# Sharing the early decode of eight weight tiles and the low parts of four token chunks between VectorE, ScalarE and TensorE

## The chip, the cores and the metric

One core of one Trainium2 chip runs the whole program. The metric is the device time of one execution in microseconds. TensorE multiplies matrices into PSUM, VectorE and ScalarE do element-wise work, GpSimd helps with small element-wise steps, SyncE (and ScalarE's sequencer) issue the DMAs.

## The reference

A gated linear attention over 4 batches, 8 heads, 768 steps and 48 channels per head is followed by two feed-forward layers on 3072 tokens (model width 384, hidden width 2048). Cut to what matters:

```python
f = 1.0 / (1.0 + np.exp(-f_logit))
for t in range(S):                      # attention
    state = f[:, :, t, :, None] * state + k_t (outer) v_t
    y[:, :, t] = q_t @ state
x = y.transpose(0, 2, 1, 3).reshape(3072, 384)
h = np.maximum(x @ w_in, 0.0);  x = (h * h) @ w_out        # layer 0
h = x @ w_in2;  x = np.where(h > 0, h, np.exp(np.minimum(h, 0)) - 1) @ w_out2   # layer 1
```

The weights reach the chip as 64-bit floats, two 32-bit words each, and are turned into 32-bit floats there ("decode").

## The kernel before

The 3072 tokens are 24 chunks of 128 (index g), and the feed-forward layers run on 12 blocks of 512 tokens (index i, six for each layer). A block goes through 16 hidden tiles of 128 (index f). One pair (i, f) is a unit. In block 0 unit f needs weight tile f of layer 0 for the first time, so all 16 tiles of layer 0 have to be loaded, decoded and split during block 0, beside the attention of the first chunks.

Products are made in a reduced format, fp32r, with every operand split in a high part (a rounded copy made by ScalarE) and a low part (the difference, made by VectorE). `up` (L403) makes nine matmuls: for each of three k the high and the low part of the weights against the high part of x, then the high parts of the weights against the low part of x. So its second matmul already needs the low part of the weights. `down` (L464) makes six matmuls of full fp32 for tiles 0 to 7 of block 0 (their second half is split later, in `split_rest`) and nine fp32r matmuls elsewhere.

A weight tile f goes through these steps, named by the letters of START where it is issued there:

- r: `load_raw` (L350), a DMA of 768 KB into one of only two buffers, so the load of tile f waits until tile f - 2 is decoded. Tiles 0 to 2 are issued by SyncE, the later ones of layer 0 by ScalarE's sequencer.
- w: `decode_weights` (L357), which calls `decode` (L50): one pass on ScalarE (L54) and three on VectorE (L56, L59, L60).
- W: `split_weights` (L373), which calls `split` (L368): high part on ScalarE (L370), low part on VectorE (L371). For tiles 0 to 7 it covers 384 columns, from tile 8 on 768.

A chunk of attention goes through f (load of the gates), q and v (loads), g (`a_gate`: tanh on ScalarE, then a scale by ScalarE or GpSimd), d (`a_decay`: two scans on VectorE), c (`a_scale`), s (`a_scores`) or, from chunk 4 on, `a_keys` (transposes tp on TensorE), t (`a_transposed`, kt on ScalarE), `a_near` (sk on TensorE), m (`a_mask`, VectorE), `a_states`, `a_far`, `a_out`, and last h (`a_hi`, L311, ScalarE) and l (`a_lo`, L318, VectorE), the high and low part of x.

The order on every engine's queue is the order of the program, written by hand: first the string START (L34), one token a step, with U, B and L for `up`, `between` (the activation) and `low` of units 0 and 1; then a loop over units u = 2, 3, ... (L569) which at each u issues what `plan[u]` holds, then `up(u)`, `down(u - 2)`, `between(u)`. `plan` is filled by `at(slot, ...)`: first the attention steps of all chunks, then, in a loop over f (L529),

```python
    for f in range(NF):
        at(f - 3, load_raw, 0, f)
        at(f - 2, decode_weights, 0, f)
        at(f - 1, split_weights, 0, f)
        if f < WHOLE:
            at(10 + f // 2, split_rest, f)
```

so that slot u holds, in this order, the split of tile u + 1, the decode of tile u + 2 and the load of tile u + 3. In slots 10 to 13 the `split_rest` of two of the tiles 0 to 7 come before these. The tensors ds (decays), mn (a running minimum of decays that in the end decides on a fallback) and dlast (the last decay of a chunk, copied by GpSimd) belong to `a_decay` (L152).

Of the kernel before, what the change touches and what calls it, by code (L numbers as in the profile page):

```python
# [11 lines left out]
F32 = mybir.dt.float32  # L12
F32R = mybir.dt.float32r
I32 = mybir.dt.int32
U32 = mybir.dt.uint32
I64 = mybir.dt.int64
AF = mybir.ActivationFunctionType
ALU = mybir.AluOpType
# [4 lines left out]
NG = NT // 128  # L23
# [8 lines left out]


START = """f0 q0 f1 I q1 M v0 f2 v1 f3 g0 q2 d0 q3 c0 g1 v2 d1 s0 r0 c1 r1 t0 g2 k0 m0 g3 s1 t1 y0 d2 c2 h0 v3 k1  # L34
m1 s2 d3 v4 t2 y1 c3 k2 m2 s3 h1 w0 t3 l0 y2 k3 m3 W0 r2 h2 q4 w1 y3 f4 l1
l2 h3 l3 W1 g4 r3 w2 U0 B0 L0 W2 d4 U1 B1 L1 w3 r4 T f5"""
STAGED = 27
WHOLE = 8
NEAR = dict(zip(range(B, NG), (4, 6, 9, 11, 19, 21, 23, 25, *range(28, 4 * NG - 23, 4))))
# [20 lines left out]
    V.scalar_tensor_tensor(out=out, in0=lo, scalar=29, in1=out, op0=ALU.logical_shift_right, op1=ALU.bitwise_or)  # L60


def chunked(ctx, tc, ff, qk, vk, vz, wraw, mask, ident, flag, out):


# [15 lines left out]
    ps_a = ctx.enter_context(tc.tile_pool(name="ps_a", bufs=1, space=PSUM))  # L81

    idt = one.tile([128, 128], F32, name="idt")
    msk = one.tile([128, 128], I32, name="msk")
    lim = one.tile([ROWS, 521], F32, name="lim")
    mn = one.tile([ROWS, 2 * NP], F32, name="mn")
    mrow = one.tile([ROWS, 1], F32, name="mrow")
    ds = [one.tile([ROWS, 2, 521], F32, name=f"ds{i}") for i in range(2)]
    tri = one.tile([128, 120], I32, name="tri")[:, 0:64]
    ss = [wpool.tile([128, 2, NP, 128], F32, tag="w", name=f"ss{i}") for i in range(2)]  # L90
    sd = [one.tile([128, 2, NP, 64], F32, name=f"sd{i}") for i in range(2)]
    s0 = one.tile([ROWS, NP, 48], F32, name="s0")
    s1 = one.tile([ROWS, NP, 48], F32, name="s1")
    state = [one.tile([ROWS, NP, 48], F32, name=f"state{b}") for b in range(B)]
    dlast = [one.tile([ROWS, NP], F32, name=f"dlast{b}") for b in range(B)]

    one.tile([128, 16], F32, name="shift")
    gap.tile([128, 48], F32, name="shift2")
# [53 lines left out]
    def a_decay(g):  # L152


        a, f = ds[g % 2], st[g]["ff"]
        V.memset(lim[:, ::65], 1.0)
        V.tensor_tensor_scan(out=a[:, 0, 0:520], data0=f[:, 0:520], data1=lim[:, 0:520], initial=1.0, op0=ALU.mult, op1=ALU.max)
        V.reciprocal(out=lim[:, 65::65], in_=a[:, 0, 64::65])
        V.tensor_tensor_scan(
            out=a[:, 1, ::-1], data0=f[:, ::-1], data1=lim[:, ::-1], initial=1.0, op0=ALU.mult, op1=ALU.max  # L160
        )
        V.tensor_tensor(out=mn, in0=mn, in1=a[:, 0, 64::65], op=ALU.min)
        here = a[:, 0, 64::65].rearrange("r (p h) -> r p h", h=2)
        if g >= B:

            wc = two.tile([ROWS, NP], F32, tag="wc", name=f"wc{g}")
            G.tensor_tensor(out=wc, in0=here[:, :, 0], in1=dlast[g % B], op=ALU.mult)
            st[g]["wc"] = wc
        if g < NG - B:
            G.tensor_copy(dlast[g % B], here[:, :, 1])  # L170

    def a_scale(g):

# [73 lines left out]
    def a_direct(g):  # L247
        s = st[g]
        pool, tag = ((ps_a, "a1"), (ps_y, "y2"), (ps_y, "y0"), (ps_y, "y1"))[g]
        yp = pool.tile([128, NK, 128], F32, tag=tag, name=f"yp{g}")  # L250
        for k in range(NK):
            for p, c in ((k, 0), (NK, 48)):
                for j in range(2):
                    PE.matmul(  # L254
                        yp[64 * j:64 * j + 64, k], s["vz"][:, k, j, c:c + 64], ss[g % 2][:, at_(p, j), p],
                        start=c == 0, stop=c > 0,
                    )
        s["yp"] = yp

# [58 lines left out]
    def a_lo(g):  # L318
        i, o = where[g]
        hi, lo = (x[:, :, o:o + 128] for x in xr[i])  # L320
        if g < B:
            V.tensor_tensor(out=lo, in0=st[g]["yp"], in1=hi, op=ALU.subtract)  # L322
        else:
            V.tensor_tensor(out=lo, in0=st.pop(g)["x1"], in1=hi, op=ALU.subtract)

# [8 lines left out]
        V.tensor_tensor(out=lo, in0=x, in1=hi, op=ALU.subtract)  # L334

    def least_decay():
        V.tensor_reduce(out=mrow, in_=mn, axis=mybir.AxisListType.X, op=ALU.min)

    def raise_flag():
        tp = ps_a.tile([1, ROWS], F32, tag="a2", name="mt")  # L340
# [13 lines left out]
    def whole(layer, f):  # L354
        return layer == 0 and f < WHOLE

    def decode_weights(layer, f):  # L357

        if whole(layer, f):
            if f % 2 == 0:  # L360
                st["pair"] = wpool.tile([128, 2, 2 * DM], U32, tag="w", name=f"pair{f}")
            b = st["pair"][:, f % 2]
        else:
            b = two.tile([128, 2 * DM], U32, tag="dec", name=f"dec{layer}_{f}")
        decode(nc, raws[layer, f], b)
        raws[layer, f] = b

    def split(t, b):  # L368
# [125 lines left out]
    def at(slot, f, *args, to=plan):  # L494

        if slot > 1:
            to.setdefault(slot, []).append((f, args))
# [31 lines left out]
    for f in range(NF):  # L529
        at(f - 3, load_raw, 0, f)  # L530
        at(f - 2, decode_weights, 0, f)
        at(f - 1, split_weights, 0, f)
        if f < WHOLE:
            at(10 + f // 2, split_rest, f)

        at(STAGED + 4 * f, load_raw, 1, f)
        at(STAGED + 4 * f + 2, decode_weights, 1, f)
        at(STAGED + 4 * f + 5, split_weights, 1, f)
        at(16 * (n1 - 1) + f + 3, fetch_weights, f)
# [4 lines left out]
    units = [(i, f) for i in range(len(BLOCKS)) for f in range(NF)]  # L544
    with tc.manual_schedule():
        V.memset(lim, DMIN)
        V.memset(mn, 1.0)
        V.memset(ss[0], 0.0)
        G.memset(ss[1], 0.0)
        for a in sd:  # L550
            G.memset(a, 0.0)

        warm = ps_a.tile([128, 512], F32, tag="a2", name="warm")
        for _ in range(3):
            PE.matmul(warm, ss[0][:, 0, 0], ss[0][:, 0].rearrange("r p t -> r (p t)"), start=True, stop=True)
        steps = {
            "I": lambda: nc.sync.dma_start(out=idt, in_=ident),
            "M": lambda: nc.sync.dma_start(out=msk, in_=mask),
            "T": lambda: [nc.sync.dma_start(out=tri[c:c + 64], in_=mask[c:c + 64, 64 - c:128 - c]) for c in (0, 64)],
            "f": load_f, "q": load_qk, "v": load_v, "r": lambda f: load_raw(0, f),  # L560
            "g": a_gate, "d": a_decay, "c": a_scale, "s": a_scores, "t": a_transposed, "m": a_mask, "k": a_state,
            "y": a_direct, "h": a_hi, "l": a_lo,
            "w": lambda f: decode_weights(0, f), "W": lambda f: split_weights(0, f),
            "U": lambda f: up(0, f), "B": lambda f: between(0, f),
            "L": lambda f: low(0, f),
        }
        for o in START.split():
            steps[o[0]](*(int(c) for c in o[1:]))
        for u in range(2, len(units) + 2):  # L569

            last = units[u - 2] == (n1 - 1, NF - 1)
            todo = plan.get(u, ())
            for f, args in () if last else todo:
                f(*args)
            if u < len(units):
                up(*units[u])
            down(*units[u - 2])
            for f, args in (*(todo if last else ()), *behind.get(u, ())):
                f(*args)
            if u < len(units):  # L580
                between(*units[u])
                low(*units[u])
# [162 lines left out]
```

## Time and profile before

| | us |
|---|---|
| median of 3 runs | 896.77 |
| lowest and highest of these | 896.03 and 897.23 |
| the profiled execution | 895.2 |
| its span (first to last instruction) | 893.4 |

Busy time of the engines in the profiled execution: TensorE 870.5 us (97%), VectorE 565.1 us (63%), ScalarE 442.6 us (50%), GpSimd 279.8 us (31%). The span is 1.8 us shorter than the execution's own time; times below count from the start of the span. A row gives the start, the duration, the engine (PE is TensorE, PEld its weight loads, DVE is VectorE, ACT is ScalarE, POOL is GpSimd, SPq and ACTq the sequencers that issue DMAs), the line of the kernel, the operation, what is written from what, and in brackets how long the engine was idle before it and what ended that.

### The profile page before, as it was taken

What the parts mean: (1) busy time and instruction counts of PE and PEld (TensorE: products, weight loads), DVE (VectorE), ACT (ScalarE), POOL (GpSimd) and SP (SyncE); (2) the same over time, 40 slices, a digit from 0 to 9 for tenths busy, and PEclk for the clock granted to TensorE, in tenths of its full rate; (3) what the DMA queues carried; (4) which work ended last, traced back from release to release, by engine and by line L of the source; (5) the groups of instructions that cost most, each with busy time, mean ns of one, the idle gap of its engine ahead of it and who ended that gap; (6) DMA issues with size and microseconds to landing.
All of it is one profiled execution on the core that took longest, in us unless ns stands there. A gap on an engine that the chain in (4) does not pass through costs nothing.

```text
span 893.4 us, 15977 instructions
## 1 busy us (share of the span) xinstructions
PE 870.5 (97%) x6273; PEld 706.8 (79%) x6273; DVE 565.1 (63%) x857; ACT 442.6 (50%) x795; POOL 279.8 (31%) x245
## 2 busy tenths in 40 slices
PE   7799999999999999999999999999999999999996
PEld 5565788888888888888888888888888888888885
DVE  8899987778777877844331565565555655654543
ACT  3466854445445455544554444444444544454443
POOL 2101045343333333223323223333333323232321
PEclk8999999999999999999999999999999999999998
DMA  9655342424454433523586400100100100200001
GB/s 269 192 171 185 114 119 72 120 81 151 140 157 150 155 114 116 193 75 109 208 307 230 162 12 1 60 12 1 60 13 0 60 12 1 71 1 28 9 1 39
DMA packets 33778, 88.66 MB, mean 99 GB/s; under 512 B 5504, under 2 KB 10240, under 8 KB 33696
## 3 DMA queue, kind: packets, MB, share of 16 engines
q1 hardware_dynamic: 31824, 77.35, 26.3%
q10 hardware_dynamic: 1872, 10.22, 3.3%
q8 instruction: 50, 0.82, 0.4%
q14 instruction: 32, 0.26, 0.1%
HBM read 64.55 MB, written 22.02 MB: 97 GB/s over the span
## 4 chain that ended last, share of the span: by engine, by line
PE 88%; DVE 4%; DMA 3%; ACT 2%; SPq 1%; issue 1%; ACTq 0%; DVEq 0%
PE ph L413 41%; PE y L477 41%; DMA ff<-ff 2%; PE o L285 1%; SPq L296 1%; PE o L270 1%; PE tp L186 1%; DMA raw<-wraw 1%; PE sk_a L209 1%; DVE pair L60 1%; DVE pair L59 1%; PE sk_a L218 0%; PE sc L196 0%; DMA vk<-vk 0%; PE yp L254 0%
## 5 line engine op out<-in xcount | busy, mean ns | idle before, releaser
L460 POOL TENSOR_TENSOR gl<-gg,gh 128x512 fp32r<-128x512 f32 x175 | 234.2, 1338 | 457.7 <-PE ph L413 189.4
L477 PE MATMUL y<-gh,wf 128*128 128x512 f32 (+1 forms) x582 | 177.7, 387 | 0.0
L446 DVE SCALAR_TENSOR_TENSOR t<-r,t 128x512 f32<-128x512 f32 (+1 forms) x97 | 71.3, 735 | 154.5 <-ACT r L445 154.1
L477 PE MATMUL y<-gh,w 128*128 128x512 f32 x528 | 162.5, 389 | 0.0
L413 PE MATMUL ph<-xh,w 128*128 128x512 f32 x576 | 154.8, 403 | 3.4 <-ACT w L370 2.5
L442 ACT ACTIVATE r<-ph 128x512 f32<-128x512 f32 (+1 forms) x97 | 57.6, 593 | 181.8 <-PE ph L413 176.8
L413 PE MATMUL ph<-xh,wf 128*128 128x512 f32 (+1 forms) x582 | 146.4, 387 | 0.0
L413 PEld LDWEIGHTS ph<-xh,w 128*128 128x128 f32 x576 | 105.1, 189 | 28.2 <-ACT w L370 2.9
L477 PEld LDWEIGHTS y<-gh,wf 128*128 128x128 f32 x582 | 108.8, 188 | 22.3
L413 PEld LDWEIGHTS ph<-xh,wf 128*128 128x128 f32 x582 | 108.6, 188 | 22.3
L477 PEld LDWEIGHTS y<-gh,w 128*128 128x128 f32 x528 | 99.1, 188 | 20.6
L477 PE MATMUL y<-gl,wf 128*128 128x512 f32 (+1 forms) x291 | 112.6, 387 | 0.0
L477 PE MATMUL y<-gl,w 128*128 128x512 f32 x264 | 102.7, 389 | 0.0
L434 ACT ACTIVATE r<-ph 128x512 f32<-128x512 f32 x88 | 52.1, 592 | 95.6 <-PE ph L413 88.9
L413 PE MATMUL ph<-xl,w 128*128 128x512 f32 x288 | 81.5, 392 | 0.6 <-DVE xl L322 0.6
L413 PE MATMUL ph<-xl,wf 128*128 128x512 f32 (+1 forms) x291 | 81.1, 387 | 0.0
L440 DVE TENSOR_TENSOR gh<-r 128x512 fp32r<-128x512 f32 x64 | 44.0, 688 | 55.2 <-ACT r L434 51.6
L447 DVE SCALAR_TENSOR_TENSOR gg<-ph,t 128x512 f32<-128x512 f32 (+1 forms) x97 | 66.6, 686 | 10.4 <-DVE t L446 0.5
L413 PEld LDWEIGHTS ph<-xl,w 128*128 128x128 f32 x288 | 54.4, 189 | 12.8 <-DVE xl L322 1.0
L477 PEld LDWEIGHTS y<-gl,wf 128*128 128x128 f32 x291 | 54.6, 188 | 11.1
L413 PEld LDWEIGHTS ph<-xl,wf 128*128 128x128 f32 x291 | 54.4, 188 | 11.1
L444 ACT ACTIVATE t<-r 128x512 f32<-128x512 f32 (+1 forms) x97 | 61.0, 629 | 3.1
(101 smaller groups left out, 1019.1 us busy)
## 6 DMA issues: line engine op xcount, KB each, us to landing
raw<-wraw SPq DMA_DIRECT2D x19, 768.0 KB, 5.8
wst<-w SPq DMA_DIRECT2D x16, 768.0 KB, 4.3
wf<-wst SPq DMA_DIRECT2D x16, 768.0 KB, 4.6
raw<-wraw ACTq DMA_DIRECT2D x13, 768.0 KB, 4.2
ff<-ff SPq DMA_DIRECT2D x22, 227.9 KB, 4.6
k<-qk SPq DMA_DIRECT2D x22, 224.0 KB, 4.7
q<-qk SPq DMA_DIRECT2D x22, 224.0 KB, 4.8
x2d<-yo SPq DMA_DIRECT2D x18, 256.0 KB, 2.9
```

What stands on the lines that cost most here:

```text
L59: V.scalar_tensor_tensor(out=out, in0=hi, scalar=0x80000000, in1=out, op0=ALU.bitwise_and, op1=ALU.bitwise_or)
L60: V.scalar_tensor_tensor(out=out, in0=lo, scalar=29, in1=out, op0=ALU.logical_shift_right, op1=ALU.bitwise_or)
L186: PE.transpose(tp[:, p, 0:ROWS], k[:, p], idt[:ROWS, :ROWS])
L413: PE.matmul(ph, w[:, a, 0, 128 * k:128 * k + 128], b[:, k, c], start=(m == 0), stop=(m == len(todo) - 1))
L434: A.activation(r[:, c], ph, AF.Relu)
L440: V.tensor_tensor(out=gh[:, c], in0=r[:, c], in1=r[:, c], op=ALU.mult)
L442: A.activation(r[:, c], ph, AF.Relu, scale=-1.0)
L444: A.activation(t[:, c], r[:, c], AF.Tanh, scale=-0.5)
L446: V.scalar_tensor_tensor(out=t[:, c], in0=r[:, c], scalar=1.0, in1=t[:, c], op0=ALU.add, op1=ALU.mult)
L447: V.scalar_tensor_tensor(out=gg[:, c], in0=ph, scalar=0.0, in1=t[:, c], op0=ALU.max, op1=ALU.add)
L460: G.tensor_tensor(out=gl, in0=gg, in1=gh, op=ALU.subtract)
L477: PE.matmul(yp_[i][m][:, c], w[:, 128 * m:128 * m + 128], b[:, c], start=(f == 0 and n_ == 0), stop=(f == NF - 1 and n_ == 2 and c.stop == n),
```

## The change

- `decode_shared` takes the place of `decode` for tiles 0 to 7. ScalarE makes a second pass: it reads byte 3 of each low word and writes its three top bits, as an integer, back into the low word. VectorE is left with two passes: shift the first pass left by 3 and OR in these bits, then OR in the sign. The first of VectorE's three passes (L56) is gone.
- `a_lo` for chunks 0 to 3: three matmuls of 128 columns with a negated identity matrix (nid, written once by ScalarE at step N) add minus the high part to what is still in PSUM, and ScalarE copies the result. VectorE's subtraction (L322) is gone. For this `a_direct` starts its accumulation once for a whole bank.
- In `plan` the decode and load of a slot now come before its splits: slot u holds the decode of tile u + 2, the load of tile u + 3, then `split_rest`, then the split of tile u + 1. This holds for all 16 tiles of layer 0.
- START: N is new, l0 moves behind q4, l1 before y3, w1 behind y3.
- mn and dlast become one tensor, `ends`, with a column group for each chunk: VectorE copies where it took a minimum, GpSimd's copies are gone, and the minimum is taken once at the end, over 192 columns in place of 8.

```diff
-m1 s2 d3 v4 t2 y1 c3 k2 m2 s3 h1 w0 t3 l0 y2 k3 m3 W0 r2 h2 q4 w1 y3 f4 l1
-l2 h3 l3 W1 g4 r3 w2 U0 B0 L0 W2 d4 U1 B1 L1 w3 r4 T f5"""
+m1 s2 d3 v4 t2 y1 c3 k2 m2 s3 h1 w0 t3 N y2 k3 m3 W0 r2 h2 q4 l0 l1 y3 w1 f4 l2
+h3 l3 W1 g4 r3 w2 U0 B0 L0 W2 d4 U1 B1 L1 w3 r4 T f5"""
...
+def decode_shared(nc, raw, out):
+    words = raw.bitcast(U32).rearrange("p (n two) -> p n two", two=2)
+    top = raw.bitcast(U8).rearrange("p (n b) -> p n b", b=8)[:, :, 3]
+    hi, lo = words[:, :, 1], words[:, :, 0]
+    A, V = nc.scalar, nc.vector
+    A.activation(out.bitcast(F32), hi.bitcast(F32), AF.Copy, scale=2.0**-112)
+    A.activation(lo, top, AF.Copy, scale=1 / 32, bias=-31 / 64)
+    V.scalar_tensor_tensor(out=out, in0=out, scalar=3, in1=lo, op0=ALU.logical_shift_left, op1=ALU.bitwise_or)
+    V.scalar_tensor_tensor(out=out, in0=hi, scalar=0x80000000, in1=out, op0=ALU.bitwise_and, op1=ALU.bitwise_or)
...
-        V.tensor_tensor(out=mn, in0=mn, in1=a[:, 0, 64::65], op=ALU.min)
-        here = a[:, 0, 64::65].rearrange("r (p h) -> r p h", h=2)
+        V.tensor_copy(ends[:, g], a[:, 0, 64::65])
         if g >= B:
+            here, last = (ends[:, i].rearrange("r (p h) -> r p h", h=2) for i in (g, g - B))
-            G.tensor_tensor(out=wc, in0=here[:, :, 0], in1=dlast[g % B], op=ALU.mult)
+            G.tensor_tensor(out=wc, in0=here[:, :, 0], in1=last[:, :, 1], op=ALU.mult)
-        if g < NG - B:
-            G.tensor_copy(dlast[g % B], here[:, :, 1])
...
         if g < B:
-            V.tensor_tensor(out=lo, in0=st[g]["yp"], in1=hi, op=ALU.subtract)
+            yp = st[g]["yp"]
+            for k in range(NK):
+                PE.matmul(yp[:, k], nid, hi[:, k], start=False, stop=True, skip_group_check=True)
+            A.activation(lo, yp, AF.Copy)
...
-        decode(nc, raws[layer, f], b)
+        (decode_shared if whole(layer, f) else decode)(nc, raws[layer, f], b)
...
         at(f - 2, decode_weights, 0, f)
+    for f in range(NF):
         at(f - 1, split_weights, 0, f)
...
+            "N": lambda: A.activation(nid, idt, AF.Copy, scale=-1.0),
```

## Rows read from the trace of the kernel before

**Rows 1.** Busy time by stage: PE, PEld, DVE, ACT, POOL, clock, DMA share, GB/s

```profile
46.00:75.00 29.00, 28.41 (x280) 17.81 (x279) 26.90 (x46) 16.51 (x31) 4.06 (x6) 1.00 0.57 193
75.00:107.00 32.00, 29.20 (x410) 20.98 (x410) 31.27 (x52) 25.62 (x52) 1.35 (x2) 1.00 0.44 149
170.00:250.00 80.00, 80.00 (x838) 66.20 (x837) 61.23 (x91) 40.46 (x81) 33.45 (x31) 1.00 0.45 140
```

**Rows 2.** Timeline of TensorE's weight loads, one that waits for a low part

```profile
99.94 1.00 PEld L413 LDWEIGHTS ph<-xh,w 128*128 128x128 f32 x5 [0.63 <-DVE w L371]
```

**Rows 3.** Groups by shape, VectorE, 22 to 112: busy us, mean ns, idle before

```profile
L371 DVE TENSOR_TENSOR w<-pair,w 128x384 fp32r<-128x384 f32 x16 | 8.5, 553 | 1.7 <-ACT w L370 1.7
...
L56 DVE TENSOR_SCALAR pair<-pair 128x768 uint32<-128x768 uint32 x8 | 4.5, 557 | 2.4 <-ACT pair L54 2.4
...
L322 DVE TENSOR_TENSOR xl<-yp,xh 128x384 fp32r<-128x384 f32 x4 | 2.0, 548 | 0.0
```

**Rows 4.** Groups by shape, ScalarE, 22 to 112

```profile
L54 ACT ACTIVATE pair<-raw 128x768 f32<-128x768 f32 x8 | 7.2, 897 | 0.0
...
L370 ACT ACTIVATE w<-dec 128x768 fp32r<-128x768 f32 x7 | 5.9, 840 | 2.5 <-DVE dec L60 1.3 <-DVE lim L156 1.1
...
L316 ACT ACTIVATE xh<-yp 128x384 fp32r<-128x384 f32 x3 | 1.5, 485 | 1.2 <-PE yp L254 1.2
...
L245 ACT ACTIVATE state<-kv 112x192 f32<-112x192 f32 x2 | 0.7, 331 | 4.7 <-PE kv L244 4.7
```

**Rows 5.** Chain that ended last, 20 to 46, in order of time

```profile
26.66 0.33 SPq L352
...
28.16 5.44 DMA ff<-ff
...
35.09 0.57 DVE pair L56
```

**Rows 6.** Timeline of VectorE around slot 2

```profile
38.23 0.56 DVE L371 TENSOR_TENSOR w<-pair,w 128x384 fp32r<-128x384 f32 x1 [0.59 <-ACT w L370]
...
45.61 0.55 DVE L371 TENSOR_TENSOR w<-pair,w 128x384 fp32r<-128x384 f32 x1
...
47.66 0.96 DVE L60 SCALAR_TENSOR_TENSOR pair<-raw,pair 128x768 uint32<-128x768 uint32 x1
```

**Rows 7.** Timeline of TensorE, units 2 to 5

```profile
38.25 3.09 PE L413 MATMUL ph<-xh,w 128*128 128x512 f32 x6 [2.49 <-ACT w L370]
...
46.12 1.64 PE L413 MATMUL ph<-xh,w 128*128 128x512 f32 x6
...
57.51 0.57 PE L186 MATMUL tp<-idt,k 112*128 112x112 f32 x4 [0.54 <-issue]
...
63.59 0.22 PE L209 MATMUL sk_h<-q,k 48*64 48x64 f32 x1
```

**Rows 8.** Timeline of ScalarE, slot 5

```profile
58.12 0.54 ACT L231 ACTIVATE kt<-tp 128x448 f32<-128x448 f32 x1 [1.13 <-PE tp L186]
58.56 0.63 ACT L146 ACTIVATE ff<-ff 112x521 f32<-112x521 f32 x1
```

**Rows 9.** Timeline of VectorE, slots 4 to 11

```profile
57.33 0.55 DVE L371 TENSOR_TENSOR w<-pair,w 128x384 fp32r<-128x384 f32 x1
...
64.58 0.43 DVE L236 COPY_PREDICATED sd<-tri,sk_a 128x256 f32<-128x256 int32 x1
...
73.89 0.96 DVE L371 TENSOR_TENSOR w<-dec,w 128x768 fp32r<-128x768 f32 x1 [0.45 <-ACT w L370]
...
98.93 0.95 DVE L371 TENSOR_TENSOR w<-dec,w 128x768 fp32r<-128x768 f32 x1
```

**Rows 10.** Timeline of TensorE, slot 13

```profile
105.93 0.72 PE L285 MATMUL o<-sd,vk 64*48 64x64 f32 x32 [1.24 <-ACT seen L277]
```

**Rows 11.** Busy time by microsecond around unit 2; columns as in the first group

```profile
40.00:41.00 1.00, 1.00 (x4) 0.81 (x3) 0.93 (x3) 0.68 (x2) 0.70 (x2) 0.50 0.86 295
...
42.00:43.00 1.00, 1.00 (x4) 0.60 (x3) 0.96 (x2) 0.00 (x0) 0.70 (x1) 0.97 0.38 91
```

More of the change, by code (lines that the diff above doesn't have):

```diff
@@ L15 @@
 U32 = mybir.dt.uint32
+U8 = mybir.dt.uint8
 I64 = mybir.dt.int64
@@ L83, in chunked @@
     idt = one.tile([128, 128], F32, name="idt")
+    nid = one.tile([128, 128], F32R, name="nid")
     msk = one.tile([128, 128], I32, name="msk")
     lim = one.tile([ROWS, 521], F32, name="lim")
-    mn = one.tile([ROWS, 2 * NP], F32, name="mn")
+    ends = one.tile([ROWS, NG, 2 * NP], F32, name="ends")
     mrow = one.tile([ROWS, 1], F32, name="mrow")
     ds = [one.tile([ROWS, 2, 521], F32, name=f"ds{i}") for i in range(2)]
-    tri = one.tile([128, 120], I32, name="tri")[:, 0:64]
+    tri = one.tile([128, 96], I32, name="tri")[:, 0:64]
     ss = [wpool.tile([128, 2, NP, 128], F32, tag="w", name=f"ss{i}") for i in range(2)]
@@ L94, in chunked @@
     state = [one.tile([ROWS, NP, 48], F32, name=f"state{b}") for b in range(B)]
-    dlast = [one.tile([ROWS, NP], F32, name=f"dlast{b}") for b in range(B)]
     one.tile([128, 16], F32, name="shift")
@@ L255, in a_direct @@
                         yp[64 * j:64 * j + 64, k], s["vz"][:, k, j, c:c + 64], ss[g % 2][:, at_(p, j), p],
-                        start=c == 0, stop=c > 0,
+                        start=k == 0 and c == 0, stop=c > 0, skip_group_check=True,
                     )
@@ L336, in least_decay @@
     def least_decay():
-        V.tensor_reduce(out=mrow, in_=mn, axis=mybir.AxisListType.X, op=ALU.min)
+        V.tensor_reduce(out=mrow, in_=ends.rearrange("r g n -> r (g n)"), axis=mybir.AxisListType.X, op=ALU.min)
     def raise_flag():
@@ L546, in chunked @@
         V.memset(lim, DMIN)
-        V.memset(mn, 1.0)
         V.memset(ss[0], 0.0)
```

## The prediction

> **What bounds the kernel now.** I read the busy time by stage first. From 170 us on TensorE is busy all the time (80.00 of 80.00 us in the stretch shown), so what happens there at other engines costs nothing, and the change hardly touches it. Between 46 and 107 us it is different: VectorE is busy 26.90 of 29 and 31.27 of 32 us, while TensorE loses 0.6 and 2.8 us [rows 1]. The timeline of VectorE in that stretch runs without gaps but for a few waits of half a microsecond. So block 0 goes at VectorE's pace, and a microsecond that TensorE gets earlier through block 0 is kept to the end; after 107 us it can't be won any more.
>
> The second thing to see is the point of handover. `up` of a unit needs the low part of its weight tile at its second matmul, and TensorE waits for exactly that: at 99.94 a weight load waits 0.63 us for L371 [rows 2]. There are five such waits (units 2, 7, 12, 14 and 15), and in units 3 to 5 and 8 the low part ends within 0.3 us of its use, as at 45.61 + 0.55 = 46.16 against unit 3, whose first matmul starts at 46.12 [rows 6, 7]. So VectorE hands over just in time, and the order of its steps counts as much as their sum.
>
> The third is what sets the start of unit 2. The chain of waits goes: decode 0 ends, SyncE issues the load of tile 2 at 26.66, then the gates of chunk 4 at 28.16, which land after 5.44 us; the tanh on them is ahead of decode 2 on ScalarE, so VectorE gets decode 2 only at 35.09 [rows 5].
>
> **The change, part by part.**
>
> *Removed from VectorE.* Eight passes L56 of 557 ns, with the gap of 0.03 us between instructions 0.59 us each, 4.7 us in all, and four subtractions L322 of 548 ns, 2.2 us [rows 3]. Tiles 0 to 2 and the four subtractions lie ahead of unit 2, the other five passes (2.95 us) behind it.
>
> *Added on ScalarE.* Eight passes of 768 elements. No row shows a read of single bytes or a write to every second word. The nearest are L54, which reads every second word (897 ns), and L370, which does neither (840 ns) [rows 4]. The strided read costs 0.06 us, a strided write as much again at most: 0.84 to 0.95 us; I take 0.90. Four copies like L316 (485 ns) and step N, which is smaller than L245 (331 ns), are added where ScalarE waits 4.7 us for L244 in two places [rows 4]. TensorE's twelve small matmuls each move a quarter of the columns of those at 46.12 (1.64 us for six), so they are under 0.27 us each, and TensorE waits 2.49 us ahead of unit 2 [rows 7]; they are hidden, and cost at most what is left of 3.3 us were that wait gone.
>
> *Start of unit 2.* Decode 0 has no cover: its path becomes two ScalarE passes and two VectorE passes. 0.90 replaces 0.59, and ScalarE passes overlap by 0.1, so it ends 0.2 us later. The load of tile 2 and the gates of chunk 4 are queued behind it on SyncE, so the tanh comes 0.2 later, and decode 2 repeats the loss: unit 2 starts 0.39 us later (0.3 to 0.6 by the bounds). That the four subtractions are gone gains nothing, since the gates end last: VectorE waits there in either order (2.4 us ahead of L56, most of it here [rows 3]).
>
> *Order in a slot.* This is the step that counts. In slot 2 VectorE ran the low part of tile 3 (45.61 to 46.16) and then decode 4 (to 47.66 + 0.96 = 48.62) [rows 6]. One decode behind the handover is thus 2.46 us, or 1.87 without L56. Now decode 4 comes first. Low part of tile 3: 46.16 + 0.39 - 0.59 (decode 3) + 1.87 = 47.83. The second matmul of unit 3, ready at 46.12 + 0.27 before, comes 1.46 us later. From there TensorE has no slack: units 3 and 4 follow, and tp(5), which had waited 0.54 us for k at 57.51 [rows 7], now starts at 56.97 + 1.46 = 58.43, 0.92 later. On ScalarE kt(5) and the tanh of chunk 6 (58.12 and 58.56 [rows 8]) shift with it, and both are queued ahead of decode 7. So its two passes start at 58.56 + 0.92 + 0.57 = 60.05 and end at 61.75. VectorE has finished the low part of tile 5 at 57.33 + 0.55 = 57.88 [rows 9], + 0.39 - 3 x 0.59 + 1.87 = 58.37, and stands still for 3.4 us: all that the dropped passes had saved. Decode 7 and the low part of tile 6 end at 64.15, and the mask of chunk 5 needs scores that TensorE ends at 63.59 + 0.22 + 0.92 = 64.73 [rows 7], against 64.58 before [rows 9]. So at the mask VectorE stands 0.15 us behind the old kernel.
>
> From tile 8 on nothing is removed, and only the order acts: each low part comes one old decode (2.46) later. What that earns is that VectorE no longer waits for ScalarE's high part (0.45 at 73.89 [rows 9]). The low part of tile 12, which ended at 98.93 + 0.95 = 99.88 [rows 9], ends at 99.88 + 0.15 + 2.46 - 0.45 = 102.04, and unit 12 is 2.1 us late.
>
> *What is given back.* In slot 13 TensorE waited 1.24 us for ScalarE's copy `seen` [rows 10], which stood behind splits and the activation of unit 12. With TensorE 2.1 us later ScalarE is ahead of it, and I leave 0.3 of this wait, so 0.94 come back. Slot 14 has no decode left, so no further delay is added. Sum: 2.1 - 0.94, about 1.2 us later from unit 14 to the end.
>
> *The rest.* `ends`: a copy of 8 columns for a minimum of 8 columns on VectorE, one larger reduction late, beside a busy TensorE; GpSimd loses 20 small copies, and a wait is added there: wc now follows VectorE's last scan, with the gate scale of the next chunk queued behind it, which is needed only by the next scan. I cost these at nothing; were VectorE's cover gone, they would cost under 0.5 us. SyncE's and ScalarE's loads keep their order; the load in a slot is now issued ahead of the split, which can only help.
>
> **The rivals.**
>
> *VectorE's saving goes through.* If ScalarE gets decode 7 done in time (TensorE less late at tp(5)), VectorE never stands still. Then at the low part of tile 12 it has gained 2.95 us, the 0.45 above and 1.1 of its 1.7 us of waits for high parts (0.59 of these at 38.23 are ahead of unit 2 [rows 3, 6]), and lost 0.39 and the 2.46 of the order: 1.65 us earlier, up to 2.6 with the wait for `seen`. I take 2.2: 894.6 us. For it: VectorE is the bound. Against it: the handover, which is just in time already.
>
> *The clock falls again.* This one is slower. TensorE stood still for 2.49 us ahead of unit 2, and the granted clock then read 0.50, its lower level (1.2 GHz), until about 42 [rows 7, 11]; six matmuls of unit 2 took 3.09 us against 1.64 in unit 3 [rows 7]. In the forecast TensorE stands still for about 2 us ahead of unit 3's second matmul and as long in unit 7, where low part 7 now follows decode 8. If the clock falls there, each fall costs 3.09 - 1.64 = 1.45 us at most, and the first is passed on through tp(5) in full: 1.2 + 1.45, 899.4 us; with both 900.9. It decides from the point where such a pause makes the clock fall; the row shows that 2.5 us did. The Trainium skill (TensorE: Matmul & The Clock Gate, section "What's actually happening") says that the reduced clock is the default and activity lifts it, so pauses bring it back. By that rule this rival would be likely, and the trace agrees with its 0.50 behind the pause ahead of unit 2.
>
> *The change acts only in the first eight tiles.* Were the new order harmless because TensorE has slack, only the 0.39 us would be left: 897.2 us. Rows 2 speak against it. It lies in the forecast's own spread.
>
> **How the numbers follow.** The profiled execution took 895.2 us, 1.8 more than its span; plus 1.2 that makes 896.4. The median of the runs is 896.77, 1.6 above it, so I forecast 898.0 for the median. About 0.2%, 1.8 us, is what a measurement of this kernel can tell from no change. The forecast has a chance of 0.50; with its spread of about 1 us, 0.46 of it are within 0.2% and 0.04 above. The clock rival has 0.31, all of it slower. The rival in which the saving goes through has 0.19, faster. That makes faster 0.19, same 0.46, slower 0.35. The range reaches from the fast rival to both falls of the clock: 894.4 to 900.9; the forecast alone would be 897.0 to 899.0.
>
> **What would show it.** In the profile after: VectorE's busy time lower by about 6.6 us; unit 2 starts at 38.6; TensorE waits for L371 about 1.5 us in unit 3 and 2 us in unit 7; VectorE idles about 3 us ahead of decode 7, released by ScalarE; unit 14 starts about 1.2 us later. The forecast is wrong if ScalarE's new pass is much dearer than 0.95 us, if VectorE has no idle time at decode 7, or if the granted clock reads 0.50 behind 45 us.

## The result, and the profile after

| | us |
|---|---|
| median before, beside it | 896.40 (895.92 to 897.23) |
| median after | 906.54 (905.24 to 907.83, 4 runs) |
| after to before | 1.0111, interval 1.0099 to 1.0124 |
| the profiled execution after, its span | 906.96, 905.2 |

The changed kernel is about 10 us slower. The forecast was 898.0, and the range ended at 900.9.

The page of after, its span and the busy time of each engine, gives the first reading. VectorE has 4.5 us less to do than before (565.1), ScalarE 8.5 more (442.6), and TensorE is busy 6.6 us longer (870.5) with twelve small matmuls more and otherwise the same work.

```profile
span 905.2 us, 15994 instructions
PE 877.1 (97%) x6285; PEld 713.3 (79%) x6285; DVE 560.6 (62%) x844; ACT 451.1 (50%) x808; POOL 265.5 (29%) x225
```

The stages of after, with the columns of [rows 1]: from 46 to 75 us VectorE falls from 26.90 to 22.22 us of work and TensorE from 28.41 to 25.78. Most of that work isn't gone, it comes later. The stretch behind 170 us is full, as before. The granted clock, third column from the end, reads 0.94 and 0.95 where it was 1.00, and 0.93 behind 107 us. In the kernel before TensorE was full there, at 1.00, as the line behind these shows.

```profile
46.00:75.00 29.00, 25.78 (x262) 15.88 (x261) 22.22 (x39) 17.33 (x32) 1.84 (x3) 0.94 0.47 156
75.00:107.00 32.00, 29.66 (x345) 20.32 (x345) 28.76 (x47) 22.73 (x44) 1.00 (x2) 0.95 0.48 159
107.00:130.00 23.00, 18.79 (x131) 14.72 (x132) 15.03 (x23) 15.39 (x31) 0.63 (x1) 0.93 0.34 107
170.00:250.00 80.00, 80.00 (x957) 66.23 (x956) 59.42 (x93) 39.95 (x83) 29.96 (x27) 1.00 0.41 129
```

```profile
107.00:130.00 23.00, 22.99 (x103) 18.51 (x102) 18.19 (x27) 14.80 (x28) 5.40 (x6) 1.00 0.36 106
```

In slices of 1 and 4 us the clock is at its lower level (0.50, 1.2 GHz) in three places that were at full clock before: behind the starts of units 3, 7 and 14. The two slices of 4 us mix both levels, hence 0.67 and 0.71.

```profile
51.00:52.00 1.00, 1.00 (x4) 0.81 (x3) 1.00 (x2) 1.00 (x2) 0.00 (x0) 0.50 0.67 221
...
76.00:80.00 4.00, 3.96 (x10) 2.67 (x11) 3.01 (x5) 3.31 (x5) 0.63 (x1) 0.67 0.94 321
...
120.00:124.00 4.00, 2.70 (x7) 2.17 (x8) 3.19 (x5) 1.26 (x3) 0.00 (x0) 0.71 0.80 242
```

TensorE's timeline shows what stands ahead of each: its second matmul of units 3, 7 and 14 waits for the low part of the weights, 1.48, 2.25 and 2.33 us (L387 is the low part; at 49.24 the trace names L170, VectorE's next instruction). L429 is `up`. A fourth pause, the 2.32 us ahead of the second matmul of unit 12 (at 108.62), was followed by no fall of the clock. In the line of unit 13's output (L297) the wait for `seen` is down to 0.26 us, from 1.24 in [rows 10].

```profile
49.24 1.86 PE L429 MATMUL ph<-xh,w 128*128 128x512 f32 x5 [1.48 <-DVE lim L170]
...
76.04 1.43 PE L429 MATMUL ph<-xh,w 128*128 128x512 f32 x5 [2.25 <-DVE w L387]
...
108.62 1.43 PE L429 MATMUL ph<-xh,w 128*128 128x512 f32 x5 [2.32 <-DVE w L387]
...
113.62 0.72 PE L297 MATMUL o<-sd,vk 64*48 64x64 f32 x32 [0.26 <-ACT seen L289]
121.30 2.17 PE L429 MATMUL ph<-xh,w 128*128 128x512 f32 x5 [2.33 <-DVE w L387]
```

VectorE's waits between 40 and 117 us (engine and line, what released it, total us, times, longest) sum to 11.5 us. In the kernel before they sum to 2.7 us in the same stretch, none longer than 0.6. So VectorE does less work in a longer time, and it waits for ScalarE's passes of a decode (L55 in tiles from 8 on, L72 is the new second pass) and for scores from TensorE (sk_h). L57 and L73 are VectorE's first pass behind these, L248 is the mask.

```profile
DVE dec L57 <- ACT dec L55: 4.8, 4, 2.4
DVE sd L248 <- PE sk_h L230: 3.5, 2, 2.2
DVE pair L73 <- ACT raw L72: 2.6, 1, 2.6
DVE w L387 <- ACT w L386: 0.6, 1, 0.6
```

### The profile page after: what moved, and what is told of

Same layout as the page of the kernel before. It is cut to its first block, busy times and chain, and to the rows that moved or that the text cites. A ratio compares the mean times of both kernels' runs of the same rounds, so it can differ in the third digit from the quotient of the medians.

```text
span 905.2 us, 15994 instructions
## 1 busy us (share of the span) xinstructions
PE 877.1 (97%) x6285; PEld 713.3 (79%) x6285; DVE 560.6 (62%) x844; ACT 451.1 (50%) x808; POOL 265.5 (29%) x225
## 4 chain that ended last, share of the span: by engine, by line
PE 92%; DVE 4%; ACT 1%; DMA 1%; issue 1%; SPq 0%; ACTq 0%; DVEq 0%
PE y L493 43%; PE ph L429 43%; PE o L282 1%; PE o L297 1%; PE tp L198 1%; DMA ff<-ff 1%; PE sk_a L221 1%; DVE w L387 1%; PE sk_a L230 1%; PE sc L208 1%; PE yp L266 0%; DVE dec L60 0%; DVE ds L171 0%; DVE pair L73 0%; PE sk_h L230 0%
## 5 line engine op out<-in xcount | busy, mean ns | idle before, releaser
L429 PE MATMUL ph<-xh,w 128*128 128x512 f32 x576 | 156.5, 406 | 12.4 <-DVE w L387 7.5
L429 PE MATMUL ph<-xh,wf 128*128 128x512 f32 (+1 forms) x582 | 146.5, 387 | 0.0
L429 PEld LDWEIGHTS ph<-xh,w 128*128 128x128 f32 x576 | 105.8, 190 | 37.4 <-DVE w L387 9.3
L429 PEld LDWEIGHTS ph<-xh,wf 128*128 128x128 f32 x582 | 108.7, 188 | 22.2
L429 PE MATMUL ph<-xl,w 128*128 128x512 f32 x288 | 83.2, 398 | 0.0
L429 PE MATMUL ph<-xl,wf 128*128 128x512 f32 (+1 forms) x291 | 81.1, 387 | 0.0
L429 PEld LDWEIGHTS ph<-xl,w 128*128 128x128 f32 x288 | 55.5, 193 | 12.1
L429 PEld LDWEIGHTS ph<-xl,wf 128*128 128x128 f32 x291 | 54.4, 188 | 11.1
```

The source lines that it names most:

```text
L429: PE.matmul(ph, w[:, a, 0, 128 * k:128 * k + 128], b[:, k, c], start=(m == 0), stop=(m == len(todo) - 1))
```

## The experiments

The question was which part of the change costs the 10 us, and in what form: through the clock, through VectorE's late low parts, or through the work that went to ScalarE and TensorE. Times are medians, ratios are to the kernel before, run beside each.

**The change with the old order of a slot.** The split stands ahead of the decode again, all else is the change.

```diff
         at(f - 2, decode_weights, 0, f)
-    for f in range(NF):
         at(f - 1, split_weights, 0, f)
```

> The changed kernel with the order of a slot put back (split of tile u+1 ahead of the decode of tile u+2); ScalarE's extra pass, the low parts through TensorE and START stay. Theory 'order': the loss of 10 us lies in the new order (each handover of a low part waits for one more decode, and for the ScalarE pass ahead of that decode), so this run comes back to 893.5 to 898 us, TensorE's waits for a low part in units 3 to 14 drop from about 9 us to under 3, and the granted clock does not read 0.50 behind 46 us. Theory 'ScalarE': the second pass on ScalarE lengthens the path of each decode, and the loss stays: over 902 us, with VectorE waiting for the new pass in slots 2 to 5.

Measured 895.95, ratio 0.9996 (0.9986 to 1.0006). The loss is gone, TensorE's waits for a low part are down to 0.4 us from 40 to 127 us, and the clock doesn't fall behind 46 us. Nothing is gained either, although VectorE stays relieved of the eight passes and the four subtractions.

**The order alone**, on the kernel before.

```diff
         at(f - 2, decode_weights, 0, f)
+    for f in range(NF):
         at(f - 1, split_weights, 0, f)
```

> The kernel before with nothing but the new order of a slot (decode of tile u+2 and load of tile u+3 ahead of the split of tile u+1). Theory 'order': 903 to 909 us, with the start of unit 2 as before (38.2 us), waits of 1.5 to 2.5 us for a low part in units 3, 7, 12 and 14, and a granted clock of 0.50 behind at least two of them. Theory 'ScalarE': within 2 us of before, 895 to 899.

Measured 906.31, ratio 1.0105 (1.0088 to 1.0122): the whole loss, without one pass moved to another engine. TensorE's waits between 40 and 127 us have this line, where before has 0.2 us, once, and the clock falls to 0.50 at the same three units as in the changed kernel:

```profile
PE ph L413 <- DVE w L371: 8.1, 5, 2.3
```

**The shared decode alone**, with the old order, and `a_lo`, `ends` and START as before.

```diff
-        decode(nc, raws[layer, f], b)
+        (decode_shared if whole(layer, f) else decode)(nc, raws[layer, f], b)
```

> The kernel before with ScalarE's second pass for tiles 0 to 7 (decode_shared) and nothing else. Theory 'order': the extra pass costs 0.4 us at the start of unit 2 and saves VectorE five passes of 0.59 us behind it, so 893.5 to 897 us. Theory 'ScalarE': over 899 us.

Measured 895.38, ratio 0.9991 (0.9982 to 1.0001). Together with the first kernel this shows what the relief of VectorE is worth: at most 0.2%, and both intervals include no change.

**The change, with TensorE kept at work in the pauses.** Ahead of `up` in units 3, 7, 12 and 14 of block 0 it repeats the first matmul six times into the tile that it is about to overwrite.

```diff
             ph = pool.tile([128, c.stop - c.start], F32, tag=tag, name=f"ph{i}_{f}_{c.start}")
+            if i == 0 and f in (3, 7, 12, 14):
+                for _ in range(6):
+                    PE.matmul(ph, w[:, 0, 0, 0:128], xh[:, 0, c], start=True, stop=True)
```

> The changed kernel with six more matmuls ahead of up in units 3, 7, 12 and 14 of the first block (each repeats the first matmul and is overwritten by it), 1.4 us of work in waits of 1.5 to 2.3 us. Where the three falls of the clock behind 46 us cost time of their own (1.6 us each), and the pauses cause them, this run is 2 to 5 us faster than the changed kernel, 901.5 to 904.5 us, and the clock stays at full behind 46 us. Where the falls are hidden behind VectorE, it is within 1 us of it, 905.5 to 907.5.

Measured 902.28, ratio 1.0070 (1.0053 to 1.0087), 4.3 us less than the changed kernel. In its stages the granted clock is 1.00 throughout:

```profile
46.00:75.00 29.00, 27.97 (x277) 18.13 (x278) 23.19 (x40) 17.59 (x32) 2.26 (x4) 1.00 0.55 178
75.00:107.00 32.00, 29.37 (x352) 20.27 (x350) 29.51 (x48) 23.78 (x47) 0.58 (x2) 1.00 0.43 139
107.00:130.00 23.00, 21.81 (x153) 17.29 (x152) 15.46 (x24) 15.44 (x31) 0.63 (x1) 1.00 0.33 101
```

So the three falls of the clock cost 4.3 us by the medians, 1.4 each, and some 5.9 us remain at full clock. The spans of the two traces differ by 5.2 us, but unit 2 began 1.65 us earlier in this one; if all of that was passed on, 3.5 are left for the clock, 1.2 each. So a fall cost between 1.2 and 1.4 us. This kernel is the clean one to read the order in, and the section behind this one does. Its unit 2 begins at 38.20, within 0.05 us of the kernel before.

**Which engine's order.** Two kernels take the new order apart, both without the shared decode. In the first ScalarE runs its pass of decode u + 2 ahead of the high part of tile u + 1, and VectorE keeps the old order (with "s" only ScalarE's step of a decode or split is issued; `decode_rest` issues VectorE's passes, `split_low` VectorE's low part):

```diff
-        at(f - 3, load_raw, 0, f)
-        at(f - 2, decode_weights, 0, f)
+        at(f - 2, decode_weights, 0, f, "s")
+    for f in range(NF):
         at(f - 1, split_weights, 0, f)
...
+    for f in range(NF):
+        if f >= 4:
+            at(f - 2, decode_rest, f)
+        at(f - 3, load_raw, 0, f)
```

> The kernel before with the new order on ScalarE alone: in a slot its pass of the decode of tile u+2 stands ahead of the high part of tile u+1, while VectorE keeps the low part of tile u+1 ahead of its three passes. Theory 'VectorE's order' (the handover of the low part waits for a decode): no loss, 895 to 898 us. Theory 'ScalarE's order' (the high part is late behind a pass that waits for its load): over 900 us.

Measured 897.07, ratio 1.0011 (1.0002 to 1.0021). In the second ScalarE has the old order, the high part first, and VectorE the new one:

```diff
+        if f >= 3:
+            at(f - 1, split_weights, 0, f, "s")
+    for f in range(NF):
         at(f - 3, load_raw, 0, f)
         at(f - 2, decode_weights, 0, f)
-        at(f - 1, split_weights, 0, f)
+    for f in range(NF):
+        if f >= 3:
+            at(f - 1, split_low, f)
```

> The counterpart: the kernel before with the new order on VectorE alone. ScalarE makes the high part of tile u+1 ahead of its pass of tile u+2, VectorE decodes tile u+2 ahead of the low part of tile u+1. Theory 'VectorE's order': the whole loss, 904 to 908 us. Theory 'ScalarE's order': under 899 us.

Measured 912.12, ratio 1.0179 (1.0162 to 1.0197), which is above the range of both theories. VectorE's order alone makes the loss, and more than the whole of it, so ScalarE's half of the new order even helps against it. Part of the surplus may be the clock, which falls four times behind 46 us in this trace. VectorE's timeline has the longest wait at 121.56, for a pass that stands behind the high part on ScalarE:

```profile
121.56 0.56 DVE L56 TENSOR_SCALAR dec<-dec 128x768 uint32<-128x768 uint32 x1 [4.47 <-ACT dec L54]
```

**Which slots.** Three kernels use the new order in some slots only, with the decode of the kernel before: slots 6 to 13; slots 4, 6, 9, 11 and 13, where VectorE has a mask, or ScalarE the copies of a chunk's output, to wait for; and slots 2, 3, 5, 7, 8, 10 and 12.

```diff
+        for h in (decodes + splits if u >= 6 else splits + decodes):
+            at(u, *h)
```

(`u in (4, 6, 9, 11, 13)` and `u in (2, 3, 5, 7, 8, 10, 12)` in the other two.)

> The kernel before with the new order in slots 6 to 13 alone (decodes of tiles 8 to 15). If most of the loss builds up there, where each decode is the old one and TensorE reaches unit 14 last, 901 to 906 us, with the start of unit 6 as before. If the loss is laid down in slots 2 to 5, under 899 us.

> The kernel before with the new order in slots 4, 6, 9, 11 and 13 alone, those in which VectorE's queue holds a mask (or ScalarE's the last copies of a chunk) that waits for TensorE. Theory 'ring' (the low part stands behind a step that waits for TensorE and, in the new order, behind a decode after that step, so the lateness of one unit makes the next handover late): most of the loss, over 901 us. Theory 'sum' (each slot with the new order costs alike): about 5 parts in 12 of the 10 us, 899 to 901.

> The kernel before with the new order in slots 2, 3, 5, 7, 8, 10 and 12 alone, in which VectorE waits for nothing of TensorE ahead of the split. Theory 'ring': the lateness is taken back in the next slot of the old order, 896 to 900 us. Theory 'sum': 7 parts in 12 of the loss, 901 to 904.

Measured 903.27, ratio 1.0070 (1.0046 to 1.0094) for the late slots; 908.18, 1.0133 (1.0110 to 1.0157) for the five; 900.18, 1.0051 (1.0036 to 1.0065) for the seven. The late slots were expected to leave the start of unit 6 as before; in their trace, the slowest of four runs from 900.25 to 905.91, unit 2 begins 1.71 us later than before with its load and unit 6 1.69 us later, so not all of that trace's loss comes from the late slots. The parts do not add up to the whole, and they can't: where a slot in the new order follows one in the old, two decodes stand ahead of one low part, which is worse than either order. Both the five and the seven have such a change of order five times, so these two may be compared with each other, and the five cost three times as much (11.9 against 3.9 us above the kernel before). Part of this is the clock again, which falls three times behind 46 us in the trace of the five and once in that of the seven; by an estimate of 1.4 us each 7.7 and 2.5 us are left. So a slot doesn't cost the same wherever it is, as the theory "sum" has it; the five cost more and the seven a little less than that theory said, while for "ring" the five lie within and the seven 0.2 us above what was expected. In the trace of the five, VectorE stands still at the mask of slot 6:

```profile
69.29 0.44 DVE L236 COPY_PREDICATED sd<-tri,sk_a 128x256 f32<-128x256 int32 x1 [4.84 <-PE sk_h L218]
```

**Taking away VectorE's wait for ScalarE's pass.** The theory "ring" says: VectorE's late low part makes TensorE late, TensorE's late output makes ScalarE's copies of it late, ScalarE's decode pass stands behind these, and VectorE waits for the pass with the next low part behind it. If so, issuing the pass at the head of the slot, ahead of these copies, should win part of the loss back. The first kernel does this with ScalarE's pass, the second with the whole decode, both in the new order with the decode of the kernel before.

```diff
+    for f in range(NF):
+        at(f - 2, decode_weights, 0, f, "s")
     for g in range(B, NG):
...
-        at(f - 2, decode_weights, 0, f)
+    for f in range(NF):
         at(f - 1, split_weights, 0, f)
```

(with `decode_rest` at the old place in the first, and right behind the pass in the second)

> The kernel before with the new order on both engines, but ScalarE's pass of the decode stands at the head of its slot, ahead of the attention's copies (kt, seen, x) and of the tanh. Theory 'ring': in the new order the low part waits for a decode whose ScalarE pass stands behind copies that wait for TensorE, which waits for the low part of the slot before, so that each lateness comes round again; with the pass at the head the ring is cut, VectorE's waits for it in slots 10 to 13 (4 us) go, and the run takes 899 to 904 us. Theory 'sum' (only the 2.46 us of VectorE's decode ahead of the handover count, and the pauses): no change, 905 to 908 us.

> The kernel before with the new order, but the whole decode of tile u+2 (ScalarE's pass and VectorE's three) stands at the head of its slot, ahead of the attention steps; the split of tile u+1 stays last. Every low part still follows one more decode, as in the new order, but no decode lies between a mask that waits for TensorE and the low part. Theory 'ring': most of the loss goes, 896 to 902 us, and VectorE's waits for scores and for ScalarE's pass in slots 4 to 13 drop from about 10 to under 4 us. Theory 'sum' (a decode ahead of each handover costs the same wherever in the slot it stands): 904 us or more.

Measured 907.29, ratio 1.0129 (1.0112 to 1.0146), and 909.21, 1.0148 (1.0133 to 1.0164). Neither wins anything back, and both times are those that the theory "sum" had expected, not "ring". In the first, VectorE's wait for the pass does fall, to 0.7 us, but another comes in its place: the waits of the stretch and ScalarE's timeline show the pass of decode 15 held back by VectorE, since its target has only two buffers, and `seen` behind it on ScalarE, for which TensorE waits.

```profile
DVE dec L59 <- ACT dec L55: 0.7, 2, 0.4
...
PE o L288 <- ACT seen L280: 3.5, 2, 2.7
```

```profile
113.88 0.90 ACT L55 ACTIVATE dec<-raw 128x768 f32<-128x768 f32 x1 [1.66 <-DVE w L383]
114.80 0.23 ACT L280 ACTIVATE seen<-o 48x4 f32<-48x4 f32 x2
```

In the second, ScalarE's pass at the head waits 3.33 us for the load of its own raw tile and 3.59 us for the low part that frees its buffer, and TensorE waits 4.90 us for `seen` behind the latter:

```profile
82.64 0.90 ACT L55 ACTIVATE dec<-raw 128x768 f32<-128x768 f32 x1 [3.33 <-DMA raw<-wraw]
89.96 0.90 ACT L55 ACTIVATE dec<-raw 128x768 f32<-128x768 f32 x1 [3.59 <-DVE w L383]
...
91.52 1.16 PE L288 MATMUL o<-sd,vk 64*48 64x64 f32 x32 [4.90 <-ACT seen L280]
```

So the ring could not be cut this way, and these two kernels speak against it as far as they go: each put another wait in the place of the one that it took away. Neither theory fits all four kernels, and the ring is not shown by them. A third buffer for decoded tiles was not tried.

**A bridge ahead of unit 2.** TensorE stands still for 2.49 us ahead of unit 2 in the kernel before, and the clock is at 0.50 behind it [rows 7, 11]. Nine repeated matmuls fill this pause: first on the kernel with the shared decode alone, then with a fourth warm-up matmul at the start of the program, then on the change with the old order.

```diff
+            if (i, f) == (0, 2):
+                for _ in range(9):
+                    PE.matmul(ph, wt[0, 1][:, 0, 0, 0:128], xh[:, 0, c], start=True, stop=True)
```

> The kernel before with decode_shared and nine more matmuls ahead of unit 2 (repeats with weight tile 1 into unit 2's PSUM tile, overwritten by its first matmul), 2.0 us of work in TensorE's pause of 2.4 us. Where that pause is what lowers the clock to 0.50 in unit 2, the clock stays up and the kernel is 1 to 1.8 us faster than with decode_shared alone: 893.3 to 894.7 us. Where the clock falls for another reason, or unit 2 is bound by VectorE anyway, 895 to 896.5.

> The same with one more matmul in the warm-up at the start (4 in place of 3), so that TensorE's pause between 8 and 9.2 us is filled and the clock stays up in the attention of the first chunks. If the low clock between 12 and 18 us delays unit 2, it starts earlier than 38 us and the run is 0.5 to 2 us faster than with the bridge alone, 892 to 894; if the loads set the start of unit 2, the same as the bridge alone.

> The changed kernel with the old order of a slot and nine more matmuls ahead of unit 2 to fill TensorE's pause there, that is, everything of the change that the runs have not shown to cost time. If the gains of the bridge and of the second ScalarE pass add up as with decode_shared alone, 894 to 895.2 us, faster than the kernel before by 1 to 2 us; if the low parts through TensorE cost something, 895.2 to 896.5.

Measured 894.68, ratio 0.9988 (0.9979 to 0.9996); 894.80, 0.9986 (0.9978 to 0.9995); 895.25, 0.9992 (0.9983 to 1.0001). In all three traces the clock reads 1.00 in unit 2, but in the first and the third it falls earlier instead, at 30 and at 32 us, and is back ahead of unit 2. The first two are the fastest kernels of this study, some 0.13% under the kernel before; against the shared decode alone (895.38) the bridge's 0.7 us lies within the intervals. With the extra warm-up the clock reads 1.00 in every slice up to 134 us: from 12 to 16 us too, where it was 0.50 before, and ahead of unit 2; unit 2's own matmuls still start at 39.82, as the stretches and TensorE's timeline show:

```profile
12.00:16.00 4.00, 2.64 (x38) 2.34 (x40) 3.79 (x9) 2.82 (x6) 1.87 (x2) 1.00 1.04 244
...
36.00:40.00 4.00, 2.44 (x11) 1.80 (x10) 2.23 (x3) 3.09 (x6) 0.27 (x1) 1.00 0.65 215
```

```profile
39.82 1.44 PE L430 MATMUL ph<-xh,w 128*128 128x512 f32 x4
```

## Why the prediction was wrong

**"So block 0 goes at VectorE's pace."** VectorE is the busiest engine there, but that does not make a microsecond of its work a microsecond of time. The shared decode alone takes eight of its passes away, five of them behind unit 2, and by the ratio 0.8 us are gained, no more than can be told from no change. Part of the answer stood in [rows 1], where TensorE loses 0.6 and 2.8 us in these stages, and in its waits from 40 to 127 us in the trace of before: 2.4 us are for `seen` on ScalarE, 0.8 for VectorE's scaled keys (L180), and 0.2 for a low part.

```profile
PE o L285 <- ACT seen L277: 2.4, 3, 1.2
PE tp L186 <- DVE k L180: 0.8, 1, 0.8
...
PE ph L413 <- DVE w L371: 0.2, 1, 0.2
```

What VectorE hands over just in time doesn't wait for VectorE alone. The rival in which the saving goes through, with 2.2 us for it, falls with this.

**The costs of single operations** held. ScalarE's pass took 901 ns (0.90 taken, 0.84 to 0.95 as bounds), the copy that replaces the subtraction 489 ns:

```profile
L72 ACT ACTIVATE raw<-raw 128x768 uint32<-128x768 uint8 x8 | 7.2, 901 | 0.0
```

VectorE's busy time fell by 4.5 us, not 6.6; 1.9 of the rest is in the subtraction for the later chunks (L324, then L340), whose mean went from 1087 to 1181 ns over 20.

**The start of unit 2.** It came at 39.85, not 38.6, but not by the change. The gates of chunk 4 were issued at 28.89 and took 6.14 us to land, against 5.44 in [rows 5]. In the kernel with the filler, which has the same program up to there, the load took 5.07 us and unit 2 began at 38.20; with the new order alone, without the new pass, unit 2 began at 39.65. The chains of waits of the two:

```profile
28.89 6.14 DMA ff<-ff
```

```profile
28.30 5.07 DMA ff<-ff
```

The landing of this one load moves unit 2 more than the 0.39 us of the step. Half of the term can still be told apart. From the landing of this load to the start of unit 2 it takes 4.63 to 4.66 us in the nine traces without the new pass and without a bridge, and 4.82 to 4.83 us in the four with it: decode 2 costs 0.18 us more, near the 0.2 of the step. The other half, decode 0 ahead of the issue, can't be seen: the issue comes between 28.07 and 29.30 us in traces with and without the new pass.

**The order, as far as unit 5,** went as worked out, once the clock is left aside. With the filler, tp(5) starts at 58.47 (predicted 58.43), and unit 5 starts 0.93 us later than before (predicted 0.92), as TensorE's timeline has it. That it agrees to 0.05 us is in part luck: the step had unit 2 0.39 us later than before, while it was 0.05 earlier here, and VectorE lost about 0.5 us in slot 2 that the step had not: one pass took 1.42 us, where the longest there had taken 1.26 before, and another waited 0.33 us for ScalarE's new pass.

```profile
58.47 0.55 PE L198 MATMUL tp<-idt,k 112*128 112x112 f32 x4
58.78 1.41 PE L432 MATMUL ph<-xh,w 128*128 128x512 f32 x4
```

**"From tile 8 on nothing is removed, and only the order acts"** is the step that failed. It is the term of the sum that was mis-sized: 2.1 us late at unit 12 and 1.2 from unit 14 on. With the filler, at full clock, the low part of tile 12 ends 5.6 us later than before (105.45 against 99.88), and units 15 and 16 start about 7 us later. The spans of these two traces differ by 6.6 us in the end, the medians by 5.9. The first matmul of `up` of some units in the two traces, before and with the filler:

| unit | before | with filler | later by |
|---|---|---|---|
| 5 | 57.85 | 58.78 | 0.93 |
| 6 | 64.64 | 65.80 | 1.16 |
| 9 | 82.57 | 85.38 | 2.81 |
| 11 | 95.13 | 98.46 | 3.33 |
| 13 | 106.57 | 111.15 | 4.58 |
| 15 | 115.01 | 122.18 | 7.17 |
| 16 | 119.39 | 126.26 | 6.87 |

TensorE's timelines have unit 15 in these lines, before and with the filler:

```profile
115.01 1.82 PE L413 MATMUL ph<-xh,w 128*128 128x512 f32 x6
```

```profile
122.18 1.52 PE L432 MATMUL ph<-xh,w 128*128 128x512 f32 x6
```

The shift isn't fixed, it grows. VectorE's timeline of the kernel with the filler shows where:

```profile
61.74 0.96 DVE L73 SCALAR_TENSOR_TENSOR pair<-pair,raw 128x768 uint32<-128x768 uint32 x1 [2.56 <-ACT raw L72]
...
65.47 0.45 DVE L248 COPY_PREDICATED sd<-tri,sk_a 128x256 f32<-128x256 int32 x1 [1.30 <-PE sk_h L230]
...
75.32 0.56 DVE L57 TENSOR_SCALAR dec<-dec 128x768 uint32<-128x768 uint32 x1 [0.98 <-ACT dec L55]
...
93.29 0.56 DVE L57 TENSOR_SCALAR dec<-dec 128x768 uint32<-128x768 uint32 x1 [0.37 <-ACT dec L55]
...
101.10 0.56 DVE L57 TENSOR_SCALAR dec<-dec 128x768 uint32<-128x768 uint32 x1 [1.14 <-ACT dec L55]
...
104.50 0.95 DVE L387 TENSOR_TENSOR w<-dec,w 128x768 fp32r<-128x768 f32 x1
...
113.78 0.56 DVE L57 TENSOR_SCALAR dec<-dec 128x768 uint32<-128x768 uint32 x1 [2.39 <-ACT dec L55]
```

VectorE's idle time ahead of decode 7 was foreseen (2.56, predicted 3.4). The mask of chunk 5 begins at 65.47, 0.74 later than predicted: the step took the scores' row at 63.59 where the last products before the mask end at 64.25, and unit 5's own wait for its low part was left out. From tile 8 on VectorE waits 0.98, 0.37 and 1.14 us more for ScalarE's passes, where the step had no wait at all. The low part of tile 12 thus ends at 104.50 + 0.95 = 105.45. Predicted was 102.04; of the difference of 3.4 us these four make 3.2 (0.74 + 0.98 + 0.37 + 1.14).

ScalarE's timeline says what each of the three passes stood behind:

```profile
73.85 0.64 ACT L160 ACTIVATE ff<-ff 112x521 f32<-112x521 f32 x1 [3.88 <-DMA ff<-ff]
...
92.36 0.91 ACT L55 ACTIVATE dec<-raw 128x768 f32<-128x768 f32 x1 [1.09 <-DVE w L387]
...
98.58 0.38 ACT L305 ACTIVATE x<-o 48x256 f32<-48x256 f32 x1 [1.16 <-PE o L297]
```

The first stands behind the tanh, which waits for a load of gates; SyncE issued that load at 70.69, 1.15 us later than before, right behind the transfers of TensorE's late output. The second waits for a buffer that VectorE's own late low part frees. Only the third stands behind the copies of TensorE's late output directly.

**"Slot 14 has no decode left, so no further delay is added"** failed beside it. The low part of tile 14 stands in slot 13, behind decode 15. ScalarE's timeline in that slot shows why decode 15 is late: the copies of x wait for TensorE's output, and the pass stands behind them.

```profile
111.26 1.57 ACT L305 ACTIVATE x<-o 48x256 f32<-48x256 f32 x4 [0.75 <-PE o L297]
112.85 0.89 ACT L55 ACTIVATE dec<-raw 128x768 f32<-128x768 f32 x1
```

VectorE stands still for 2.39 us, then decodes tile 15, and only then makes the low part of tile 14, which ends at 117.18 + 0.95. In the kernel before the low part came first, so a late pass held up only a decode that nobody needed yet. This is what the step did not see: with the low part behind the decode, each wait of the decode becomes a wait of TensorE, and TensorE's lateness comes back through the output, ScalarE's copies and the pass. The way back is not always this one, as the three passes above show: one came by SyncE's queue and one from a buffer. What is given back at `seen` was right in itself (0.26 against the 0.3 left), and small. The traces show these links one by one, and the kernels with one engine's order show that VectorE's half of the order is the cause. That the lateness goes round and so grows is read from the traces and not shown by an experiment, since the two kernels that should have cut the circle won nothing back.

**The clock** stood at nothing in the forecast's own sum. The rival had its mechanism, its place and its price right: 1.45 us at most for each fall, 1.2 to 1.4 measured, in units 3 and 7 and in a third that was not foreseen, unit 14. Its 900.9 us with both falls is still 5.6 short, since it stood on the order's 1.2 us. The row that it went by had a pause of 2.5 us; the runs show that 1.48 us could be enough, and that 2.32 us ahead of unit 12 did not do it, so the length of the pause alone does not decide. The Trainium skill (TensorE: Matmul & The Clock Gate, section "What's actually happening") says that activity lifts the clock from its reduced default; the filler agrees with this, since TensorE, kept at work, stayed at 1.00.

The 10.1 us thus are about 4.3 of the clock and 5.9 of the order by the medians, of which 1.2 were in the forecast. The rest of the change, the part that gave it its name, is worth nothing that these runs can measure.

## What to carry to other kernels

Where one engine hands over just in time to another, count the order on its queue ahead of its load: a step that is needed next must not stand behind one that can itself wait, and a late handover should be followed round the whole circle of engines before it is called a fixed shift. An engine that is busy nearly all of a stage is not yet the bound of it; ask what the engine that sets the end waits for, and how long. A forecast that puts new pauses into TensorE's work, here of 1.5 us and more, has to price the clock with them.

## What the runs showed of the hardware

Three pauses of TensorE (1.48, 2.25 and 2.33 us), in work that was otherwise dense, were followed by stretches at 0.50 of the clock, each worth 1.2 to 1.4 us; a fourth of 2.32 us was not. Repeated matmuls into a tile about to be overwritten kept the clock at 1.00 in the kernel with the filler, at no cost that shows. A full clock from 12 to 16 us and ahead of unit 2 won nothing that shows over the bridge alone (894.80 against 894.68); unit 2 started with its load. The same load of gates took between 5.07 and 6.59 us to land in the thirteen traces without a bridge, and unit 2 started between 38.20 and 39.96, always 4.63 to 4.83 us behind the landing. A pass of ScalarE that reads one byte in eight and writes every second word took 901 ns, against 897 ns for one that only reads every second word [rows 4].
